# GpSimd's background instructions cut into pieces of at most 384 elements, in a fused H3 and squared-ReLU MLP kernel

## The chip, the cores and the metric

The kernel runs on one core of a Trainium2 chip. The metric is the device time of one execution in microseconds. Engines are named as in the profile: PE (TensorE, matrix products; PEld is its weight loads), DVE (VectorE), ACT (ScalarE), POOL (GpSimd) and SP (SyncE, which here issues every DMA from one queue, in order).

## The reference

Two layers, each of a block A (H3, a gated long convolution) and a block B (an MLP), in float32, with S = 2048 tokens, D = 1024 channels, F = 3584:

```
A(q):  k_shift = causal depthwise conv of k with shift_k (4 taps)
       kv = k_shift * v
       y  = causal conv of kv with ssm_k (2048 taps, per channel, by FFT) + kv * ssm_D
       return q * y
B(x):  h = x @ w1 + b1;  r = where(h > 0, h, 0);  h = r * r
       return h @ w2 + b2

x = q
for layer in 0, 1:
    x = x + A(layernorm(x))
    x = x + B(layernorm(x))
```

k, v and the filters do not depend on x, so the long convolution y is computed once and used in both layers.

## The kernel before, in words

Tokens come in four blocks b of 512. The work of the MLPs is a list of 8 units (layer, block) in the order (0,0), (1,0), (0,1), (0,2), (1,1), (0,3), (1,2), (1,3), called u0 to u7 here. A unit is a list of steps; one step uses one weight tile of 128x512 for 12 matmuls of 512 columns. Each float32 operand is split into a high and a low part, and a product is three matmuls (lines L336, L337, L338 of `mm3`).

Each step needs its weight tile `whl` split first: ACT copies the high part (`w_hi`, L1013), and the low part is a subtraction `wr - high` (`w_lo`, L1021) on DVE, or, where u0 passes into u1, three times in four on POOL. Split tiles of some weights are kept in DRAM (`wd_m...`) and come back by a DMA straight into `whl` (L1011). There are 6 `whl` buffers.

Beside the MLP steps runs the long convolution for blocks 1 to 3 (sb = 1, 2, 3), in the background. A transform (`fwd_x`, `fwd_g`, mostly ACT and DVE with some matmuls on PE; L366, L368, L484 and L485 are DVE's, L421 a transpose on PE) writes spectra to DRAM. `prod_stream` reads them into `cx` and `cg` and forms, for each of 16 channel groups, 3 kinds and 2 output positions per sb, the products of j+1 blocks of 128 elements: `mult` on POOL (L526) writes `cp` (3 buffers), and two products later in the program `red` on DVE (L530) sums it into `sm`. j is 2 and 3 for sb = 1, 4 and 5 for sb = 2, 6 and 7 for sb = 3. When a group's sums are there, POOL folds them (`fold`, L676) and makes a butterfly (L680, L681), and inverse matmuls on PE (L596, first stage) follow.

Near the start of each unit the bias b2 is loaded as a row over all partitions into a `px` buffer (2 buffers) and added by POOL to the accumulators that hold the residual: `add_b2` (L1744, four adds of 1024 elements) in u0 to u4, `add_b2w` (L1601, eight adds of 512) in u5 to u7. The `px` buffers also serve the loads of x for the next unit (`load_x`, L726).

The order of each engine's instructions is the order in which the program emits them: the step loop emits the MLP step and then, by a pace of products per step, background work. Only the first block (up to about 125 us) is ordered by a planner. So every engine works through a fixed queue, and an instruction that waits holds all behind it on the same engine; on SP that goes for DMA issues too.

Of the kernel before, what the change touches and what calls it, by code (L numbers as in the profile page):

```python
# [18 lines left out]
S, D, F = 2048, 1024, 3584  # L19
P = 128  # L20
# [7 lines left out]
BL = 256  # L28
# [15 lines left out]
NORM_0 = "VA"  # L44
AHEAD_0 = 4
BURST = 1.06
FIN = "GGG"
PACE_SLACK = {1: 74, 3: 10}
PACE_TO = {1: 2}
# [191 lines left out]
def tile_h3_mlp(ctx: ExitStack, tc: tile.TileContext, q, kT, vT, shk, ssmT, ssmD, w1, b1, w2, b2,  # L241
                fwd_t, pro_t, inv_t, sgn_t, out):
    nc = tc.nc
    V, A, G, PE, SY = nc.vector, nc.scalar, nc.gpsimd, nc.tensor, nc.sync
# [275 lines left out]
    def prod_stream():  # L520
# [2 lines left out]

        def mult(st, xt, gt, j):
            pr = cv.tile([P, CU, j + 1], F32, name="cp", bufs=3)
            G.tensor_mul(pr.rearrange("p c i -> p i c"), xt[:, 0:j + 1], gt[:, j::-1])  # L526
            st["pr"] = pr

        def red(st, sm, ty, jj):
# [2 lines left out]
        def fin(st, sm, sb, g, k):  # L532
            s = sm.rearrange("p k j c -> p k (j c)")
            E = ENG[FIN[sb - 1]]
            if k == 0:
                fold(E, s)
                lag.at(1, fin, st, sm, sb, g, 1)
            elif k == 1 and sb <= PLAIN:
# [100 lines left out]
        for n, (sb, g, ty) in enumerate(units):  # L639
            while n not in when:  # L640
                if (sb, g // 2) in fwd_done:
                    load(n)
                else:
                    lag.tick()
                    yield None
            while lag.n < when[n] + 2:
                lag.tick()
                yield None
            if ty == 0:
                while sums[0] - sums[1] >= 2:  # L650
                    lag.tick()
                    yield None
                sums[0] += 1
                sm = cv.tile([P, 3, BT, CU], F32, name="sm", bufs=2)
                if g % 2 == 0:
                    pair = {}
            for jj in range(BT):
                j = BT * sb + jj
                st = {"pair": pair}
                mult(st, *got[n], j)  # L660
                lag.at(2, red, st, sm, ty, jj)
                if jj == BT - 1:
                    if ty == 2:
                        lag.at(3, fin, st, sm, sb, g, 0)
                    fill(n)
                lag.tick()
                yield (j + 1) * CU * 1e-3
# [5 lines left out]
        return t[:, e].rearrange("p (n c) -> p n c", c=CG)  # L673

    def fold(E, s):
        E.tensor_add(s[:, 1:3], s[:, 1:3], s[:, 0:1].to_broadcast([P, 2, s.shape[2]]))  # L676

    def butterfly(E, s):
        y = s[:, 1:3].rearrange("p r (j u c) -> p u (r j) c", u=2, c=CG)
# [380 lines left out]
    def first_block():  # L1060
# [27 lines left out]
        with tc.tile_pool(name="pro", bufs=1) as pro:  # L1088
# [226 lines left out]
            def prods(c, jj):  # L1315
                sm = new(cv, "sm", 2, [P, 3, 2, CU])
                xs, gs = spec["x", c], spec["g", c]
                for ty in range(3):
                    rd = [(xs, ty), (gs, ty)]
                    if jj == 0:  # L1320
                        pl.add([("G", g_cost(BL), 1), ("V", v2_cost(BL), 1)], lambda e, ty=ty: ENG[e].tensor_mul(
                            sm.t[:, ty], xs.t[:, ty, :, 0], gs.t[:, ty, :, 0]), rd, [(sm, ty)])
                        continue
                    pr = new(cv, "fx", 4, [P, T])
                    pv = lambda t: t.rearrange("p (g b c) -> p g b c", g=2, b=BT)
                    pl.add([("G", g_cost(T), 1), ("V", v2_cost(T), 1)], lambda e, ty=ty, pr=pr: ENG[e].tensor_mul(
                        pv(pr.t), xs.t[:, ty], gs.t[:, ty, :, ::-1]), rd, [pr])
                    pl.add([("V", v2_cost(BL), 1), ("G", g_cost(BL), 1)], lambda e, ty=ty, pr=pr: ENG[e].tensor_add(
                        sm.t[:, ty], pv(pr.t)[:, :, 0], pv(pr.t)[:, :, 1]), [pr], [(sm, ty)])
                fl_ = lambda: sm.t.rearrange("p k g c -> p k (g c)")  # L1330
                pl.add([("G", g_cost(T), 1), ("V", v2_cost(T), 1)], lambda e: fold(ENG[e], fl_()),
                       [(sm, 0)], [(sm, 1), (sm, 2)])
                z = {}
                pl.add([("V", 2 * v2_cost(BL), 1), ("G", 2 * g_cost(BL), 1)], lambda e: z.update(
                    enumerate(butterfly(ENG[e], fl_()))), [], [(sm, 0), (sm, 1), (sm, 2)])
                behind(c, jj, sm, lambda: (z[0], z[1]), [(sm, 0), (sm, 1)])
# [261 lines left out]
    def add_b2w(st, wacc):  # L1598
        for j, h in ((1, 0), (2, 1), (3, 0), ("x", 1)):
            for a in wacc[j]:  # L1600
                G.tensor_add(a, a, st["t"][:, h * 512:(h + 1) * 512])  # L1601

    def evict_w(os, wacc, j, c):
        for n in range(2):
# [136 lines left out]

    def add_b2(st, accs):
        for a in accs:
            G.tensor_add(a, a, st["t"])  # L1744

    def store_out(accs, l, b):
        for tt in range(NT):
# [11 lines left out]
    for sb in range(1, NB):  # L1759
        if WIN[sb] > lo_u:  # L1760
# [3 lines left out]
            n = sum(last_step[u] + 1 - start_step[u] - 19 * (1 - PREP_PACE) for u in range(lo_u, hi_u))  # L1764
# [16 lines left out]
    for s, (k, u, c, a, i, tts, w) in enumerate(steps):  # L1781
# [3 lines left out]
        if u != cur_u:  # L1785
            cur_u = u
            if u:
                xT = nxt
            bst = {}
            if u in WINO:  # L1790
                wacc, rp = {}, {}
                lag.at(11, load_wacc, wacc, b)
                lag.at(34, load_b2, bst)
                lag.at(38, add_b2w, bst, wacc)
            else:
                if not (u and direct[u - 1]):
                    accs = []
                    lag.at(5, load_acc, accs, b)
                lag.at(12, load_b2, bst)
                lag.at(16, add_b2, bst, accs)  # L1800
# [10 lines left out]
        if k == "m1":  # L1811
# [9 lines left out]
            for kk in range(4):  # L1821
                t = slice(kk * P, (kk + 1) * P)
# [8 lines left out]
        elif k == "w2":  # L1831
# [7 lines left out]
            for n in range(2):  # L1839
                t = slice(n * P, (n + 1) * P)  # L1840
# [11 lines left out]
        else:  # L1852
# [5 lines left out]
            for tt in tts:  # L1858
                t = slice(tt * P, (tt + 1) * P)
# [33 lines left out]
        if u + 1 < NU and not direct[u]:  # L1893
            n = s - start_step[u]
# [23 lines left out]
        owed += rate  # L1918
        todo = min(owed, BURST * rate)
        while todo > 0:  # L1920
# [63 lines left out]
```

## Time and profile before

| | us |
|---|---|
| median of 3 runs | 2706.65 (2705.93 to 2711.74) |
| the profiled execution | 2710.68 |
| its span, first to last instruction | 2708.9 |
| PE busy | 2658.2 (98% of the span) |
| DVE busy | 1988.0 (73%) |
| ACT busy | 1124.1 (41%) |
| POOL busy | 845.8 (31%), 532 instructions |
| mean granted TensorE clock | 0.996 |

POOL's work lies almost wholly in the first 1700 us, where the convolution runs. PE is busy nearly all the time after the first 125 us, so the time is that of PE's work plus the places where PE stands still. Busy time of DVE and POOL includes time in which an instruction was started but held up.

### The profile page before, as it was taken

Reading aid. Unit: us, or ns where it says so; the run is one execution under the profiler, and the core shown is the slowest. Engines: PE = TensorE matmul, PEld = TensorE weight load, DVE = VectorE, ACT = ScalarE, POOL = GpSimd, SP = SyncE. Lnnn points to the kernel's source line nnn. Section 1 sums busy time; section 2 is a strip of 40 time slices with the busy share of each in tenths; the row PEclk is TensorE's granted clock in tenths of the full one; section 3 lists DMA queues with packets and bytes.
Section 4 is the critical chain, followed back from the end, with each engine's and each line's share of the span. In section 5 each row is a group of like instructions: output and inputs, shape, how many; then the busy total and the mean of one; then the engine's idle time right before and its main releaser. Section 6 shows DMA issues by size and latency. Waiting matters only on the chain.

```text
span 2708.9 us, 36533 instructions
## 1 busy us (share of the span) xinstructions
PE 2658.2 (98%) x12568; PEld 2227.5 (82%) x12568; DVE 1988.0 (73%) x3066; ACT 1124.1 (41%) x1936; POOL 845.8 (31%) x532
## 2 busy tenths in 40 slices
PE   7999999999999999999999999999999999999999
PEld 6888787888888888888888888888788788878887
DVE  7878888788987877779677765376787666664565
ACT  3454344433444233442234422244455444445443
POOL 2436565355632655236553454000000010001000
PEclk9999999999999999999999999999999999999999
DMA  8789898699999898788978887789888866676556
GB/s 250 262 305 314 290 311 279 234 308 372 333 305 321 300 342 285 266 334 289 354 263 276 298 304 248 237 295 310 294 286 300 278 231 212 231 270 210 179 167 206
DMA packets 377482, 755.05 MB, mean 279 GB/s; under 512 B 43840, under 2 KB 159184, under 8 KB 377296
## 3 DMA queue, kind: packets, MB, share of 16 engines
q1 hardware_dynamic: 377296, 752.72, 81.6%
q8 instruction: 99, 1.62, 0.2%
q14 instruction: 87, 0.71, 0.1%
HBM read 602.63 MB, written 149.95 MB: 278 GB/s over the span
## 4 chain that ended last, share of the span: by engine, by line
PE 82%; DMA 7%; DVE 6%; issue 2%; POOL 1%; ACT 1%; SPq 1%; DVEq 0%; ACTq 0%; POOLq 0%
PE p L336 25%; PE p L337 25%; PE p L338 25%; DMA wr<-w 2%; PE p L1097 2%; DVE whl L1021 1%; DMA whl<-wd_m 1%; PE pt L336 1%; PE pt L337 1%; PE pt L338 1%; DMA wd_m<-whl 1%; DMA whl<-wd_t 1%; DMA yt<-yd 0%; DMA wd_t<-whl 0%; DMA fx<-kT 0%
## 5 line engine op out<-in xcount | busy, mean ns | idle before, releaser
L526 POOL TENSOR_TENSOR cp<-cx,cg 128x384 f32<-128x384 f32 (+5 forms) x288 | 543.2, 1898 | 569.9 <-DVE sm L530 380.4
L336 PE MATMUL p<-xh,whl 128*128 128x512 f32 (+1 forms) x1840 | 707.6, 385 | 4.3 <-DMA whl<-wd_m 4.2
L338 PE MATMUL p<-xh,whl 128*128 128x512 f32 (+1 forms) x1840 | 703.8, 383 | 0.8 <-POOL whl L1021 0.8
L337 PE MATMUL p<-xl,whl 128*128 128x512 f32 (+1 forms) x1840 | 703.8, 383 | 0.1
L1013 ACT CAST whl<-wr 128x512 fp32r<-128x512 f32 x637 | 383.4, 619 | 437.0 <-PE p L338 308.5
L1021 DVE TENSOR_TENSOR whl<-wr,whl 128x512 fp32r<-128x512 f32 x622 | 500.9, 826 | 73.6 <-ACT whl L1013 69.2
L336 PE MATMUL p<-whl,rh 128*128 128x512 f32 x1372 | 541.2, 394 | 7.3 <-ACT whl L1013 3.7
L337 PE MATMUL p<-whl,rh 128*128 128x512 f32 x1372 | 536.6, 391 | 1.8 <-POOL whl L1021 0.8
L338 PE MATMUL p<-whl,rl 128*128 128x512 f32 x1372 | 536.0, 391 | 0.0
L336 PEld LDWEIGHTS p<-xh,whl 128*128 128x128 f32 x1840 | 347.0, 189 | 71.8 <-DMA whl<-wd_m 3.5
L338 PEld LDWEIGHTS p<-xh,whl 128*128 128x128 f32 x1840 | 346.6, 188 | 68.6 <-POOL whl L1021 1.0
L337 PEld LDWEIGHTS p<-xl,whl 128*128 128x128 f32 x1840 | 346.8, 188 | 65.6 <-DVE xl L1410 0.3
L336 PEld LDWEIGHTS p<-whl,rh 128*128 128x128 f32 x1372 | 258.7, 189 | 62.2 <-DMA whl<-wd_m 4.8
L337 PEld LDWEIGHTS p<-whl,rh 128*128 128x128 f32 x1372 | 258.7, 189 | 56.0 <-DVE whl L1021 3.4
L338 PEld LDWEIGHTS p<-whl,rl 128*128 128x128 f32 x1372 | 258.5, 188 | 54.3
L1504 DVE TENSOR_TENSOR rl<-wr,rh 128x512 fp32r<-128x512 f32 x140 | 145.8, 1042 | 178.3 <-ACT rh L1499 178.2
L1601 POOL TENSOR_TENSOR acc<-acc,px 128x512 f32<-128x512 f32 x18 | 23.2, 1325 | 766.6 <-DMA px<-b 766.6
L530 DVE TENSOR_REDUCE sm<-cp 128x128 f32<-128x384 f32 (+5 forms) x288 | 249.5, 874 | 10.9 <-POOL cp L526 10.9
L1496 ACT ACTIVATE wr<-p,b1t 128x512 f32<-128x512 f32 x138 | 95.2, 690 | 366.8 <-PE p L338 365.8
L1565 DVE TENSOR_TENSOR rl<-wr,rh 128x256 fp32r<-128x256 f32 x84 | 48.9, 582 | 211.2 <-ACT rh L1560 211.1
L1624 DVE TENSOR_TENSOR acc<-p,acc 128x512 f32<-128x512 f32 x152 | 99.8, 686 | 83.4 <-PE p L338 83.4
L1557 ACT ACTIVATE wr<-p,b1t 128x512 f32<-128x512 f32 x84 | 57.9, 689 | 191.0 <-PE p L338 190.9
(277 smaller groups left out, 3304.5 us busy)
## 6 DMA issues: line engine op xcount, KB each, us to landing
whl<-wd_m SPq DMA_DIRECT2D x379, 512.0 KB, 5.4
wr<-w SPq DMA_DIRECT2D x493, 256.0 KB, 5.4
wr<-td SPq DMA_DIRECT2D x152, 256.0 KB, 4.0
wd_m<-whl SPq DMA_DIRECT2D x70, 512.0 KB, 6.1
cx<-xd SPq DMA_DIRECT2D x48, 512.0 KB, 6.0
cg<-gd SPq DMA_DIRECT2D x48, 512.0 KB, 6.8
gd<-fg SPq DMA_DIRECT2D x72, 256.0 KB, 6.5
cx<-xd SPq DMA_DIRECT2D x48, 384.0 KB, 5.7
```

The costliest lines, as they stand in the source:

```text
L336: PE.matmul(o, lh, rh, start=start, stop=False)
L337: PE.matmul(o, lh, rl, start=False, stop=False)
L338: PE.matmul(o, ll, rh, start=False, stop=stop)
L526: G.tensor_mul(pr.rearrange("p c i -> p i c"), xt[:, 0:j + 1], gt[:, j::-1])
L530: V.tensor_reduce(sm[:, ty, jj], st["pr"], axis=AX.X, op=OP.add)
L1013: A.copy(t[:, 0], raws[n]["t"])
L1021: ENG[e[n % len(e)]].tensor_sub(t[:, 1], raws[n]["t"], t[:, 0].bitcast(F32))
L1097: PE.matmul(o, lh, r, start=start, stop=stop)
L1496: A.activation(r, st["o"], AF.Relu, bias=b1t[:, st["f"]:st["f"] + 1])
L1504: V.tensor_sub(st["lo"], st["r"]["t"], st["hi"].bitcast(F32))
L1557: A.activation(r, st["o"], AF.Relu, bias=b1t[:, st["f"]:st["f"] + 1])
L1624: V.tensor_add(accs[tt][:, d], o, accs[tt][:, d])
```

## The change

`mult` cuts a product of j+1 blocks into pieces of at most 3 blocks (384 elements): 3 blocks stay one instruction, 4, 5 and 6 blocks become two (2+2, 2+3, 3+3), 7 and 8 become three (2+2+3, 2+3+3). `fold` becomes two adds of 256 in place of one of 512. The adds of b2 are made in pieces of 256 (`BL`): four for each of 1024, two for each of 512. The arithmetic on each element is the same.

On POOL that is 336 more products, 48 more folds, and 60 and 24 more adds of b2: 468 instructions on top of 532. On every other engine and on SP the instructions and their order stay as they were, but for two folds of the first block that run on DVE and become four.

```diff
+G_BLOCKS = 3
...
         def mult(st, xt, gt, j):
             pr = cv.tile([P, CU, j + 1], F32, name="cp", bufs=3)
-            G.tensor_mul(pr.rearrange("p c i -> p i c"), xt[:, 0:j + 1], gt[:, j::-1])
+            n = -(-(j + 1) // G_BLOCKS)
+            cuts = [(j + 1) * k // n for k in range(n + 1)]
+            for a, e in zip(cuts, cuts[1:]):
+                G.tensor_mul(pr[:, :, a:e].rearrange("p c i -> p i c"), xt[:, a:e],
+                             gt[:, j - a:j - e if e <= j else None:-1])
             st["pr"] = pr
...
     def fold(E, s):
-        E.tensor_add(s[:, 1:3], s[:, 1:3], s[:, 0:1].to_broadcast([P, 2, s.shape[2]]))
+        for k in (1, 2):
+            E.tensor_add(s[:, k], s[:, k], s[:, 0])
...
     def add_b2w(st, wacc):
         for j, h in ((1, 0), (2, 1), (3, 0), ("x", 1)):
             for a in wacc[j]:
-                G.tensor_add(a, a, st["t"][:, h * 512:(h + 1) * 512])
+                for d in range(0, 512, BL):
+                    G.tensor_add(a[:, d:d + BL], a[:, d:d + BL], st["t"][:, h * 512 + d:h * 512 + d + BL])
...
     def add_b2(st, accs):
         for a in accs:
-            G.tensor_add(a, a, st["t"])
+            for d in range(0, D, BL):
+                G.tensor_add(a[:, d:d + BL], a[:, d:d + BL], st["t"][:, d:d + BL])
```

## The prediction

> **What bounds the kernel now.** I read the page first: it gives 2658.2 us of busy PE in a span of 2708.9, so the time is PE's work plus the places where PE stands still. Then the list of PE's waits, the granted clock in a few windows, and the timelines of PE, DVE, POOL and SP around the longest stalls. Rows of a list of waits read: who waited, for what, us in total, times, longest.
>
> ```profile
> PE 2658.2 (98%) x12568; PEld 2227.5 (82%) x12568; DVE 1988.0 (73%) x3066; ACT 1124.1 (41%) x1936; POOL 845.8 (31%) x532
> PE pt L421 <- DVE fx L368: 8.1, 3, 6.4
> PE p L336 <- DMA whl<-wd_m: 7.2, 6, 2.8
> PE pt L596 <- DVE fg L485: 2.7, 1, 2.7
> PE p L338 <- POOL whl L1021: 0.8, 1, 0.8
> DVE sm L530 <- POOL cp L526: 10.9, 15, 1.6
> ```
>
> After the first block PE waits little, and for DVE and DMA rather than for POOL. A change on POOL therefore acts through three doors: how long POOL holds up DVE, how late DVE gets what POOL makes, and how late SP gets a buffer that POOL frees. The last row is the second door: small, but there.
>
> A stall costs more than its length, because the clock falls behind it. Windows (length, busy time of PE, PEld, DVE, ACT and POOL, granted clock, DMA):
>
> ```profile
> 300.05 1.10 PE L421 MATMUL pt<-ident,fx 128*128 128x128 f32 x4 [6.36 <-DVE fx L368]
> 295.87:306.10 10.23, 6.05 (x17) 4.92 (x18) 9.74 (x14) 1.49 (x3) 6.73 (x6) 0.50 0.88 281
> 446.05:449.46 3.41, 3.41 (x13) 2.83 (x12) 3.38 (x7) 0.39 (x1) 2.60 (x2) 0.50 0.00 0
> 1910.36:1913.78 3.42, 3.42 (x10) 2.65 (x9) 0.00 (x0) 0.00 (x0) 0.00 (x0) 0.50 0.94 347
> ```
>
> Behind the 6.36 us stall PE runs at half speed until 306.10, 6.05 us of running, so 3.0 us are lost on top. The second window follows the 2.67 us stall of L596 (2.7 in the list), the third the 2.81 us one: 3.4 us at 0.50, 1.7 us lost each. I call the first two A (9.4 us in all) and B (4.4 us).
>
> **What a cut costs on POOL.** The same add in three lengths (duration min/median/max in ns), and two starts in a row:
>
> ```profile
> L681 POOL TENSOR_TENSOR sm<-sm x49: 725/742/1255, 109.2 to 1692.0; 128x256 f32<-128x256 f32 x49
> L1601 POOL TENSOR_TENSOR acc<-acc,px x18: 1277/1292/1540, 1891.7 to 2486.4; 128x512 f32<-128x512 f32 x18
> L1744 POOL TENSOR_TENSOR acc<-acc,px x20: 2383/2842/2877, 164.5 to 1553.4; 128x1024 f32<-128x1024 f32 x20
> 432.62 0.74 POOL L681 TENSOR_TENSOR sm<-sm 128x256 f32<-128x256 f32 x1
> 433.31 1.31 POOL L526 TENSOR_TENSOR cp<-cx,cg 128x512 f32<-128x512 f32 x1
> ```
>
> Two of 256 take 1450 ns where one of 512 takes 1277: 0.17 us more by duration. But the 0.74 us instruction is followed after 0.69, so starts overlap ends by 0.05: a cut costs 0.12 us where POOL runs on without a break. The 468 cuts add 56 us to 846 of POOL. The larger cost stands beside it: at each boundary a waiting DVE instruction may go in between. L1744's median lies 0.46 us above its minimum, which I read as that.
>
> **What a cut gives to DVE.** The low-part subtraction, all of DVE's 622:
>
> ```profile
> L1021 DVE TENSOR_TENSOR whl<-wr,whl x622: 673/685/2909, 145.3 to 2697.4; 128x512 fp32r<-128x512 f32 x156
> ```
>
> The longest exceeds the shortest by 2.24 us, about one POOL instruction of 1024. So a DVE instruction with two SBUF inputs waits for the POOL instruction that is under way, and goes next. In pieces of 256 and 384 that wait falls to 0.7 or 1.0 us at most. The Trainium skill's page "SBUF — State Buffer", section "Who interferes with whom", says that the pair of ports shared by the two engines is taken for a whole instruction by whichever issues first while the other blocks fully, also for a DVE instruction with two SBUF inputs against a POOL one that reads SBUF. The trace agrees, with those 2.24 us; the rule speaks for the change, and what it would make of the time is the second rival.
>
> **The long products (sb = 2 and 3, 550 to 1700 us): nothing.** They hold most of the cuts (288), but:
>
> ```profile
> L526 POOL TENSOR_TENSOR cp<-cx,cg 128x768 f32<-128x768 f32 (+2 forms) x193 | 415.5, 2159 | 479.0 <-DVE sm L530 357.0 <-DMA cg<-gd 110.9 <-DMA kd<-fk 6.4
> ```
>
> In that window POOL idles 479 us before products, 357 of them until DVE has emptied a buffer. POOL runs ahead, so 288 x 0.12 = 35 us plus handovers of up to 0.46 us each (132 us) fit in, and PE's longest waits lie elsewhere, so DVE's gain buys nothing. If the cover were gone, DVE's sums would come late and hold the split weights behind them.
>
> **Place 1: b2 adds at the head of u1.** POOL, DVE, then PE (start, length, engine and line, idle before):
>
> ```profile
> 531.84 10.86 POOL L1744 TENSOR_TENSOR acc<-acc,px 128x1024 f32<-128x1024 f32 x4
> 542.65 1.73 POOL L1021 TENSOR_TENSOR whl<-wr,whl 128x512 fp32r<-128x512 f32 x1
> 532.45 2.36 DVE L1504 TENSOR_TENSOR rl<-wr,rh 128x512 fp32r<-128x512 f32 x1 [5.30 <-ACT rh L1499]
> 534.73 2.90 DVE L1021 TENSOR_TENSOR whl<-wr,whl 128x512 fp32r<-128x512 f32 x1
> 537.55 5.69 DVE L1504 TENSOR_TENSOR rl<-wr,rh 128x512 fp32r<-128x512 f32 x2
> 543.17 1.76 DVE L1021 TENSOR_TENSOR whl<-wr,whl 128x512 fp32r<-128x512 f32 x1
> 544.43 0.38 PE L338 MATMUL p<-xh,whl 128*128 128x256 f32 x1 [0.83 <-POOL whl L1021]
> ```
>
> Here POOL also makes a weight's low part, queued behind the adds, and PE is already waiting 0.83 us for it. Four adds alone are 4 x 2.38 - 3 x 0.05 = 9.4 us; the row has 10.86, so three handovers at 0.49. Sixteen pieces alone are 16 x 0.725 - 15 x 0.05 = 10.85. DVE no longer loses about 2 us per instruction, so the five DVE instructions shown can all go in where three did: 5 x 0.46 = 2.3. Together 13.2 against 10.9: L1021 comes 2.3 to 2.4 us later, and PE stands 3.2 us instead of 0.83. That is longer than the 2.67 us that brought half clock, so 1.7 more: **+4.1 us**. With no more handovers than now it is +1.5 without clock loss, with seven +5.
>
> The Trainium skill's page "TensorE: Matmul & The Clock Gate", section "HAM oscillation — how this bites in real kernels", states as its rule that there be no idle gap of PE above about 3.4 us. By it, 3.2 us would pass without a slower clock, and the sum below would be 1.7 us lower. The trace differs, with half clock behind 2.67 us, and I go by the trace.
>
> **Place 2: b2 adds in u5; place 3: in u6.** SP's queue (SPq) issues a load of x into the `px` buffer that holds b2, so it stands until the last add, and the weight loads stand behind it (the first row is of SP's waits):
>
> ```profile
> SPq L726 <- POOL fk L1601: 18.1, 2, 10.0
> 1891.71 7.72 POOL L1601 TENSOR_TENSOR acc<-acc,px 128x512 f32<-128x512 f32 x6 [199.01 <-DMA px<-b]
> 1899.38 2.99 POOL L1601 TENSOR_TENSOR fk<-fk,px 128x512 f32<-128x512 f32 x2
> 1902.40 0.32 SPq L726 DMA_DIRECT2D px<-x  x1
> 1902.82 1.36 SPq L1011 DMA_DIRECT2D whl<-wd_m  x1
> 1909.27 0.50 PE L336 MATMUL p<-xh,whl 128*128 128x512 f32 x1 [2.81 <-DMA whl<-wd_m]
> 2199.76 0.32 SPq L726 DMA_DIRECT2D px<-x  x1
> 2204.76 0.19 PEld L336 LDWEIGHTS p<-xh,whl 128*128 128x128 f32 x1 [0.29 <-DMA whl<-wd_m]
> ```
>
> The adds end at 1902.37, SP goes on at 1902.40, and the load lands as PE starts at 1909.27 after 2.81 us. Eight more cuts are 8 x 0.12 = 1.0 us, and one more handover makes 1.3. That reaches PE whole: a stall of 4.1 us. Its half clock lies between the 1.7 us of the 2.8 us stall (no more than now) and the 3.0 of A; I take 0.8 more. **+2.1 us**, from +1.0 to +3. In u6 PEld waits 0.29 us for the load behind the same step, so there is no slack left: **+1.2 us**, from +0.8 to +1.6, below the stalls that move the clock. u7 loads no further unit.
>
> **The first convolution stage (sb = 1, 190 to 490 us): about even.** Stalls A and B lie here. Before A:
>
> ```profile
> 291.66 3.69 DVE L366 SCALAR_TENSOR_TENSOR fx<-fx,shkt 128x512 f32<-128x512 f32 x3
> 295.27 1.21 DVE L484 TENSOR_TENSOR fg<-fk 128x256 f32<-128x256 f32 x1
> 296.41 1.49 DVE L485 TENSOR_TENSOR fg<-fk 128x256 f32<-128x256 f32 x1
> 297.82 1.48 DVE L1021 TENSOR_TENSOR whl<-wr,whl 128x512 fp32r<-128x512 f32 x1
> 291.23 1.30 POOL L676 TENSOR_TENSOR sm<-sm 128x512 f32<-128x512 f32 x1 [3.71 <-DVE sm L530]
> 294.77 3.98 POOL L526 TENSOR_TENSOR cp<-cx,cg 128x384 f32<-128x384 f32 x3
> ```
>
> The fold holds L366 from 291.66 to 292.53; cut, to 291.96, so 0.6 us come free. But the second half is one more turn for POOL, and the three products that hold L484, L485 and L1021 (0.8 us for the last: 1.48 against 0.67) have 384 elements and stay whole. So A keeps nearly all of its 6.36 us. In this stage only the products of 512 and the folds are cut, half the instructions; what DVE saves there it partly gives back in waiting for `cp` (10.9 us in 15 waits, above). I take **-1 us**, from -14 (A and B gone) to +6. The cut adds in u0 (about 165 us) lie where PE has no stall: nothing. Two DVE folds in the first block: under 0.2 us.
>
> **Sum.** +4.1 + 2.1 + 1.2 - 1.0 = +6.4 us, set against the profiled execution's 2710.68 (span 2708.9 and 1.8 around it): 2717.1. That execution lies 4.0 above the median of the runs; the differences should hold for the median as well: 2706.65 + 6.4 = **2713.0**.
>
> **The rivals.** *POOL too slow in the first stage* (slower still): cut products of 512 cost 0.12 + 0.46 us each; where DVE already waits for `cp`, that goes to DVE. Five of the waits in the approach to A and B would be 5 x 0.58 = 2.9 us more stall, and about 3 us of clock: 2713.0 + 6 = 2719. For it, the 15 waits; against it, POOL idles there too. Chance 0.18.
>
> *The locks decide* (faster): by the whole-instruction hold, DVE loses half as much at each meeting. If that carries back through the 100 us ahead of A, DVE meets its dates: A (9.4) and B (4.4) go, 13.8 us, less half of the three places' cost (3.7): 2696.6; with A gone alone and the three places in full, 2704.7. It decides from 3.7 us of DVE time saved ahead of A, since stalls below 2.67 us are the only ones seen without a clock loss. Against it, the uncut 384s. Chance 0.24.
>
> *All hidden* (no change): DVE's earlier instructions make up for POOL's later ones at place 1, DMA timing swallows places 2 and 3: 2706 to 2709. Chance 0.16. That the change does not do what it says has no place here: POOL's queue holds the pieces, and other queues are in their old order.
>
> **Chances.** The forecast has 0.42. About 0.2% (5.4 us) is what a measurement can tell from no change. The forecast's bounds reach from +2 to +10, 0.30 above the line and 0.12 within; the first rival is slower; the locks faster by more than 0.2% in 0.22 and within it in 0.02; the last within. Slower 0.48, same 0.30, faster 0.22. Range: from 2698, leaving out the lower part of the locks' case, to 2722, the first rival with its clock loss in full.
>
> **What would show it.** Right: L1021 on POOL after the adds at the head of u1 starts 2 to 3 us later against them, with PE waiting about 3 us for POOL; the waits of SP's L726 for POOL's L1601 rise from about 18 to 21 us, and stalls before `whl<-wd_m` grow; L1021's longest on DVE falls to about 1.7 us; A still there. Wrong: A or B gone, place 1's stall unchanged, or new stalls of PE between 550 and 1700 us.

## The result and the profile after

The changed kernel takes 2715.94 us (median of 8 runs, 2712.03 to 2718.89) against 2707.78 us (8 runs, 2705.93 to 2711.74) for the kernel before on the same chip: ratio 1.0029, 95% interval 1.0018 to 1.004, that is 8.2 us slower, from 4.9 to 10.8. The forecast was 2713.0 us, slower by 6.4. In the changed kernel lines of the second half are numbered some more: L421 is L422, L526 is L530, L530 is L535, L596 is L601, L626 is L631, L726 is L732, L1011 is L1017, L1021 is L1027, L1504 is L1510, L1601 is L1608, L1744 is L1752, and L336 to L338 are L337 to L339.

The profiled execution took 2713.12 us (span 2711.3), near the lowest of this kernel's runs, while that of before (2710.68) was near the highest of its own. So the two traces differ by only 2.4 us where the medians differ by 8.2. A trace can show here where PE stands; sums are taken from the timed runs. First the page: engines, then groups (busy us, mean ns | idle us before them).

```profile
PE 2659.8 (98%) x12568; PEld 2229.0 (82%) x12568; DVE 1891.6 (70%) x3068; ACT 1126.2 (42%) x1936; POOL 950.7 (35%) x1000
L530 POOL TENSOR_TENSOR cp<-cx,cg 128x384 f32<-128x384 f32 (+1 forms) x624 | 622.0, 1029 | 503.7 <-DVE sm L535 288.8
L1027 DVE TENSOR_TENSOR whl<-wr,whl 128x512 fp32r<-128x512 f32 x622 | 470.9, 778 | 78.0 <-ACT whl L1019 75.6
L535 DVE TENSOR_REDUCE sm<-cp 128x128 f32<-128x384 f32 (+5 forms) x288 | 250.1, 875 | 40.2 <-POOL cp L530 40.2
```

DVE is busy 96.4 us less than before (1988.0), because its subtractions are held up for a shorter time (the low part takes 778 ns on the mean, 826 before; the sums, with 875 and 874 ns, gain nothing); POOL is busy 104.9 us more (845.8). DVE's wait for products rose from 10.9 to 40.2 us (most of it behind the adds of b2, see e7 and e8). None of the three shows in PE's busy time, 2659.8 against 2658.2. The list of PE's waits (total, times, longest) and the spread of DVE's low-part subtraction (ns, least/median/longest):

```profile
PE p L337 <- DMA whl<-wd_m: 9.6, 10, 2.2
PE pt L422 <- DVE fx L369: 7.2, 1, 7.2
PE p L339 <- POOL whl L1027: 3.5, 1, 3.5
PE pt L601 <- DVE fg L486: 2.3, 1, 2.3
```

```profile
L1027 DVE TENSOR_TENSOR whl<-wr,whl x622: 673/686/1548, 144.8 to 2699.5; 128x512 fp32r<-128x512 f32 x156
```

So DVE's longest hold fell from 2909 to 1548 ns, as the cut into shorter POOL instructions should make it; but the two stalls that DVE is to blame for, A (7.2 against 6.4) and B (2.3 against 2.7), are still there, and the wait for POOL's L1027 grew from 0.8 to 3.5 us. Place 1 in the timelines of POOL, DVE and PE (start, length, instruction, idle before):

```profile
528.68 14.32 POOL L1752 TENSOR_TENSOR acc<-acc,px 128x256 f32<-128x256 f32 x16
542.96 1.26 POOL L1027 TENSOR_TENSOR whl<-wr,whl 128x512 fp32r<-128x512 f32 x1
```

```profile
529.29 0.69 DVE L1510 TENSOR_TENSOR rl<-wr,rh 128x512 fp32r<-128x512 f32 x1 [5.02 <-ACT rh L1505]
530.26 0.87 DVE L1027 TENSOR_TENSOR whl<-wr,whl 128x512 fp32r<-128x512 f32 x1 [0.28 <-ACT whl L1019]
532.17 0.80 DVE L1510 TENSOR_TENSOR rl<-wr,rh 128x512 fp32r<-128x512 f32 x1 [1.04 <-ACT rh L1505]
535.00 1.23 DVE L1510 TENSOR_TENSOR rl<-wr,rh 128x512 fp32r<-128x512 f32 x1 [2.03 <-ACT rh L1505]
536.15 1.23 DVE L1027 TENSOR_TENSOR whl<-wr,whl 128x512 fp32r<-128x512 f32 x1
537.93 1.28 DVE L1510 TENSOR_TENSOR rl<-wr,rh 128x512 fp32r<-128x512 f32 x1 [0.55 <-ACT rh L1505]
539.14 0.54 DVE L535 TENSOR_REDUCE sm<-cp 128x128 f32<-128x384 f32 x1
540.77 0.97 DVE L1510 TENSOR_TENSOR rl<-wr,rh 128x512 fp32r<-128x512 f32 x1 [1.09 <-ACT rh L1505]
```

```profile
544.27 0.58 PE L339 MATMUL p<-xh,whl 128*128 128x256 f32 x1 [3.54 <-POOL whl L1027]
```

The adds take 14.32 us where they took 10.86. DVE no longer suffers: it is often idle, waiting for ACT. Its eight instructions all go in between the sixteen pieces, and POOL pays for it. What PE waits for is POOL's own subtraction, behind the last piece. Windows of after (length; busy PE, PEld, DVE, ACT, POOL; granted clock; DMA), the first behind this stall, the others behind stalls of 2.31 us (B) and 2.16 us (before `whl<-wd_m`, PE resumes at 629.27):

```profile
542.80:549.70 6.90, 5.43 (x18) 4.75 (x19) 1.47 (x3) 2.22 (x4) 6.90 (x9) 0.51 0.08 30
443.80:447.30 3.50, 3.50 (x11) 2.77 (x10) 3.47 (x6) 0.50 (x2) 2.42 (x3) 0.51 0.01 2
626.00:633.00 7.00, 4.84 (x22) 3.70 (x22) 4.17 (x6) 3.68 (x8) 5.96 (x7) 1.00 1.05 381
```

At place 1 PE runs 5.43 us at half clock, 2.7 us lost; with 3.54 - 0.83 = 2.7 us more standing, 5.4 in all. Both traces hold the same matmuls in the same order, so the starts of each can be compared, and they say nearly the same: after is 2.9 us ahead of before when the stall begins and comes out 2.3 behind, 5.2 in all.

Places 2 and 3, from the waits and timelines of after:

```profile
SPq L732 <- POOL fk L1608: 21.0, 2, 11.4
1896.31 8.56 POOL L1608 TENSOR_TENSOR acc<-acc,px 128x256 f32<-128x256 f32 x12 [200.17 <-DMA px<-b]
1904.84 2.81 POOL L1608 TENSOR_TENSOR fk<-fk,px 128x256 f32<-128x256 f32 x4
1907.67 0.32 SPq L732 DMA_DIRECT2D px<-x  x1
1908.10 0.37 SPq L1017 DMA_DIRECT2D whl<-wd_m  x1
1912.68 0.50 PE L337 MATMUL p<-xh,whl 128*128 128x512 f32 x1 [2.16 <-DMA whl<-wd_m]
2208.10 0.19 PEld L337 LDWEIGHTS p<-xh,whl 128*128 128x128 f32 x1 [1.90 <-DMA whl<-wd_m]
```

SP's wait did rise from 18.1 to 21.0 us. In u6 (last row) PEld's wait for the load rose from 0.29 to 1.90 us. But in u5 the stall became shorter, 2.16 us against 2.81: the load was issued 1908.10 - 1896.31 = 11.8 us after the start of the adds, not 11.1, yet PE went on 4.58 us after the issue, not 6.45.

### The profile page after: what moved, and what is told of

The parts are those of the page before. It is cut to its first block, busy times and chain, and to the rows that moved or that the text cites. A ratio compares the mean times of both kernels' runs of the same rounds, so it can differ in the third digit from the quotient of the medians.

```text
span 2711.3 us, 36967 instructions
## 1 busy us (share of the span) xinstructions
PE 2659.8 (98%) x12568; PEld 2229.0 (82%) x12568; DVE 1891.6 (70%) x3068; ACT 1126.2 (42%) x1936; POOL 950.7 (35%) x1000
## 4 chain that ended last, share of the span: by engine, by line
PE 76%; DMA 10%; DVE 6%; POOL 4%; issue 2%; SPq 1%; ACT 1%; DVEq 0%; POOLq 0%; ACTq 0%
PE p L338 23%; PE p L337 23%; PE p L339 23%; PE p L1103 2%; DMA whl<-wd_m 2%; DMA cg<-gd 2%; POOL cp L530 2%; DVE whl L1027 1%; DMA gd<-fg 1%; DMA wr<-w 1%; POOL acc L1752 1%; PE pt L339 1%; PE pt L337 1%; PE pt L338 1%; DMA wd_m<-whl 1%
## 5 line engine op out<-in xcount | busy, mean ns | idle before, releaser
L530 POOL TENSOR_TENSOR cp<-cx,cg 128x384 f32<-128x384 f32 (+1 forms) x624 | 622.0, 1029 | 503.7 <-DVE sm L535 288.8
L337 PE MATMUL p<-xh,whl 128*128 128x512 f32 (+1 forms) x1840 | 708.6, 385 | 7.4 <-DMA whl<-wd_m 7.3
L339 PE MATMUL p<-xh,whl 128*128 128x512 f32 (+1 forms) x1840 | 704.2, 383 | 3.5 <-POOL whl L1027 3.5
L338 PE MATMUL p<-xl,whl 128*128 128x512 f32 (+1 forms) x1840 | 704.2, 383 | 0.1
L337 PE MATMUL p<-whl,rh 128*128 128x512 f32 x1372 | 541.2, 394 | 5.9 <-ACT whl L1019 3.4
L338 PE MATMUL p<-whl,rh 128*128 128x512 f32 x1372 | 536.2, 391 | 1.6 <-POOL whl L1027 0.8
L339 PE MATMUL p<-whl,rl 128*128 128x512 f32 x1372 | 535.8, 391 | 0.0
L1027 DVE TENSOR_TENSOR whl<-wr,whl 128x512 fp32r<-128x512 f32 x622 | 470.9, 778 | 78.0 <-ACT whl L1019 75.6
L337 PEld LDWEIGHTS p<-xh,whl 128*128 128x128 f32 x1840 | 347.3, 189 | 76.3 <-DMA whl<-wd_m 4.9
L339 PEld LDWEIGHTS p<-xh,whl 128*128 128x128 f32 x1840 | 347.1, 189 | 71.2 <-POOL whl L1027 3.7
L338 PEld LDWEIGHTS p<-xl,whl 128*128 128x128 f32 x1840 | 347.3, 189 | 65.6 <-DVE xl L1416 0.3
L337 PEld LDWEIGHTS p<-whl,rh 128*128 128x128 f32 x1372 | 258.7, 189 | 60.7 <-ACT whl L1019 4.2
L338 PEld LDWEIGHTS p<-whl,rh 128*128 128x128 f32 x1372 | 258.6, 188 | 56.1 <-DVE whl L1027 3.2
L339 PEld LDWEIGHTS p<-whl,rl 128*128 128x128 f32 x1372 | 258.3, 188 | 54.3
L1608 POOL TENSOR_TENSOR acc<-acc,px 128x256 f32<-128x256 f32 x36 | 25.7, 750 | 763.8 <-DMA px<-b 763.8
L535 DVE TENSOR_REDUCE sm<-cp 128x128 f32<-128x384 f32 (+5 forms) x288 | 250.1, 875 | 40.2 <-POOL cp L530 40.2
L1510 DVE TENSOR_TENSOR rl<-wr,rh 128x512 fp32r<-128x512 f32 x140 | 118.3, 845 | 214.1 <-ACT rh L1505 213.8
```

What stands on the lines that cost most here:

```text
L337: PE.matmul(o, lh, rh, start=start, stop=False)
L338: PE.matmul(o, lh, rl, start=False, stop=False)
L339: PE.matmul(o, ll, rh, start=False, stop=stop)
L530: G.tensor_mul(pr[:, :, a:e].rearrange("p c i -> p i c"), xt[:, a:e], gt[:, j - a:j - e if e <= j else None:-1])
L535: V.tensor_reduce(sm[:, ty, jj], st["pr"], axis=AX.X, op=OP.add)
L1027: ENG[e[n % len(e)]].tensor_sub(t[:, 1], raws[n]["t"], t[:, 0].bitcast(F32))
```

## The experiments

Ratios are to the kernel before, timed on the same chip in the same rounds (medians 2707.95, 2709.77 and 2709.40 us in the three sets: e1 to e4, e5 to e8, e9 to e12), with 95% intervals.

### Which part costs: e1, e2, e3, e4

**e1**, the changed kernel with `add_b2` whole again:

```diff
-            for d in range(0, D, BL):
-                G.tensor_add(a[:, d:d + BL], a[:, d:d + BL], st["t"][:, d:d + BL])
+            G.tensor_add(a, a, st["t"])
```

> The changed kernel with the adds of 1024 left whole again (products, folds and the adds of u5 to u7 still cut). Theory, that the cut adds at the head of u1 delay a weight's low part that POOL makes behind them: the stall of PE there falls from 3.54 us to about 0.8, its half clock goes, and with them about 5.4 us: 2710.5, from 2709 to 2712. Rival, that the shorter products and folds cost the time through a POOL that is late in the convolution: 2715 to 2717, as the changed kernel.

**e2**, the kernel before with only this cut made (the same lines the other way round).

> The kernel before with the adds of 1024 alone cut into four. Theory (adds at the head of u1): that stall of PE grows from 0.83 us to 3 us or more with half clock behind it, 4 to 5.5 us: 2712 to 2713.5 against 2707.8. Rival (products): within 1 us of the kernel before.

**e3**, the kernel before with only the products cut (`mult` as in the change; folds and adds whole).

> The kernel before with the products alone cut. Theory: DVE is held less in the first convolution stage, PE gains 1 to 3 us up to 490 us, as the changed kernel's trace shows (3.4 us ahead there, part of it from the folds), and may lose 2 or 3 us to a late DMA near 620 us: 2705 to 2709. Rival (POOL late in the convolution): slower by 5 us or more, 2713 and up, with DVE waiting longer for the products.

**e4**, the kernel before with only `add_b2w` cut, in pieces of 256.

> The kernel before with the eight adds of 512 in u5 to u7 alone cut into two. Theory (they hold SP's queue, and the weight loads behind it): the adds end 1 us later, PE's stall at 1906 us grows by 1.0 to 1.3 us and one of 1.0 to 1.5 us appears at 2204: 2709 to 2711. Rival, that the load's landing is set by DMA traffic and not by its issue: within 0.7 us of the kernel before.

| | us | ratio |
|---|---|---|
| changed kernel | 2715.94 | 1.0029 (1.0018 to 1.0040) |
| e1, all but the cut of `add_b2` | 2710.59 | 1.0007 (0.9998 to 1.0016) |
| e2, the cut of `add_b2` alone | 2712.03 | 1.0015 (1.0006 to 1.0024) |
| e3, the products alone | 2707.78 | 0.9998 (0.9989 to 1.0006) |
| e4, the cut of `add_b2w` alone | 2710.22 | 1.0007 (0.9998 to 1.0016) |

Place 1 in the timelines of e1 and of e2, POOL then PE:

```profile
526.51 10.86 POOL L1751 TENSOR_TENSOR acc<-acc,px 128x1024 f32<-128x1024 f32 x4
539.10 0.39 PE L339 MATMUL p<-xh,whl 128*128 128x256 f32 x1 [0.83 <-POOL whl L1027]
```

```profile
528.63 14.43 POOL L1745 TENSOR_TENSOR acc<-acc,px 128x256 f32<-128x256 f32 x16
544.33 0.39 PE L338 MATMUL p<-xh,whl 128*128 128x256 f32 x1 [3.65 <-POOL whl L1021]
```

With the adds whole the stall is back at 0.83 us though everything else is cut; with them cut it is 3.65 us though everything else is whole. The cut of `add_b2` by itself makes the kernel 0.15% slower, 4.1 us (1.6 to 6.5), and without it the changed kernel can't be told from before. This is the largest part, and it lies at place 1. e3 shows that the products, 336 of the 468 added instructions, cost nothing that can be measured. e4's interval reaches no change, so its 1.9 us (0.0007 of 2707.95) rest on its trace, where place 3 is seen again:

```profile
2204.70 0.19 PEld L336 LDWEIGHTS p<-xh,whl 128*128 128x128 f32 x1 [1.55 <-DMA whl<-wd_m]
```

The parts together make 0.15 + 0.07 - 0.02 = 0.20%, the whole 0.29% (0.18 to 0.40). The difference lies within the intervals; the folds weren't run alone. Taken out of the changed kernel (e1) the cut of `add_b2` is worth 0.29 - 0.07 = 0.22%, put into the kernel before (e2) 0.15%.

### Who must not stand behind the adds: e5, e6

All low parts between u0 and u1 are made on DVE, so that POOL makes none behind its adds; e5 does this to the changed kernel, e6 to the one before.

```diff
-WLO = {"b": "GGGV", "x": "GGGV"}
+WLO = {"b": "GGGV", "x": "V"}
```

> The changed kernel, with the weights' low parts at the passage from u0 to u1 all made by DVE (three in four were POOL's). All pieces stay cut. Theory (a weight queued behind the cut adds on POOL): PE no longer waits for POOL there, the 3.5 us stall and its half clock go, 4 to 6 us: 2710 to 2712. Rival (the cut adds cost through DVE, which their many small pieces hold up): PE waits for DVE's L1021 there instead, 2714 to 2717.

> The same move of the low parts in the kernel before, whose adds of 1024 are whole. Theory: there is only a stall of 0.83 us to take away at that place, and DVE is held up to 2.4 us by each add: 2706 to 2710, no gain that can be measured. Rival (the move itself is a gain anywhere): 2703 to 2705.

e5: 2713.49 us, 1.0016 (1.0006 to 1.0025). e6: 2709.14 us, 0.9998 (0.9989 to 1.0007). All of e5's waits of PE between 500 and 700 us that the list has:

```profile
PE p L337 <- DMA whl<-wd_m: 2.8, 1, 2.8
PE pt L339 <- DVE whl L1027: 1.4, 1, 1.4
```

The wait for POOL is gone, as the theory of place 1 says, and a shorter one for DVE (1.4 us) takes its place; e6 has the same 1.4 us. The ratio of the cut kernel fell from 1.0029 to 1.0016, so about half of the loss went with POOL's place in that queue. By the starts of the same matmuls from 500 to 560 us, the changed kernel loses 5.2 us on the kernel before, e2 4.5, and e5, e6 and e1 nothing: in these traces the loss at place 1 went whole. What remains of e5's 0.16% lies elsewhere in its trace, where PE stands 2.8 us near 625 us and PEld 2.6 us at place 3. It is more than e1 leaves, but the two intervals overlap.

### The products apart: e7, e8

**e7** cuts only the products of sb = 1 (`n = ... if j < 4 else 1` in `mult`), **e8** only those of sb = 2 and 3 (`if j >= 4 else 1`); all else is as before.

> The kernel before with only the products of 512 (sb = 1, 190 to 560 us) cut. If cutting helps DVE in the first convolution stage: 2704 to 2707. If it makes POOL late there (as one rival of the prediction had it): 2710 to 2714. If both are small: 2707 to 2709, and no stall before a weight load near 620 us above the 0 to 1.6 us of kernels with whole products.

> The kernel before with only the products of 640 to 1024 (sb = 2 and 3, from 560 us on) cut. The prediction held these for nothing: 2707 to 2709. The traces with all products cut show a stall of PE of 2.2 to 2.4 us near 620 us before a weight load that stands behind a load for the products in SP's queue: if it comes from these cuts it is here too, and the time is 2709 to 2712.

e7: 2708.46 us, 0.9999 (0.9990 to 1.0008). e8: 2710.58 us, 1.0003 (0.9994 to 1.0012). Neither moves the time, so the nothing of e3 isn't a gain in one stage against a loss in the other. (e8's 2710.58 us lies in the range expected with a stall near 620 us, but the kernel before took 2709.77 in this set, and the stall in e8 is 0.72 us.) A is 6.6 us in e7, 6.0 in e8, 5.0 in e3; over all fourteen traces it goes from 5.0 to 7.3, in no order with what is cut. DVE's waits for products rise to 15.1 us in e7, 12.9 in e8 and 20.4 in e3. The first row is e3's, the second e2's, where every product is whole:

```profile
DVE sm L535 <- POOL cp L530: 20.4, 29, 2.5
DVE sm L530 <- POOL cp L526: 30.0, 20, 6.9
```

The cut of products makes twice the 10.9 us of before, at no cost to PE that can be measured; I take it that the waits end before a weight is late, since the program takes up a product two products after it is made. The larger part of the changed kernel's 40.2 us is not theirs: e1, with the products cut and the adds of b2 whole, has 16.7 us, and the longest waits (6.9 in e2, 7.2 in after) are for products that stand behind the cut adds near 1230 us. They cost PE nothing either: from 1000 to 1250 us it waits 0.2 us in after and 0.5 in before.

### How much per piece: e9

**e9** is the kernel before with `add_b2` in pieces of 512 (eight instead of four or sixteen).

```diff
-            G.tensor_add(a, a, st["t"])
+            for d in range(0, D, 512):
+                G.tensor_add(a[:, d:d + 512], a[:, d:d + 512], st["t"][:, d:d + 512])
```

> The kernel before with the adds of 1024 alone cut into two of 512 (not four of 256). A dose of the first theory: eight adds take 8 x 1.28 - 7 x 0.05 = 9.9 us alone, and four to six handovers of 0.46 us make 11.7 to 12.6 us where four whole adds take 10.86 and sixteen pieces 14.3 to 14.4. PE's stall for the weight behind them is 1.7 to 2.6 us (0.83 whole, 3.5 in quarters); with half clock behind it if it passes about 2.3 us: 2708.5 to 2711.5 against about 2708.5 for the kernel before. Rival (any cut there costs the full amount, by what it does to DVE): 2712 and more.

2712.02 us, 1.0006 (0.9996 to 1.0016): just above the range expected in us, and as a ratio between before and e2, with an interval that reaches both. So the time alone doesn't decide between the theory and its rival. The timeline of e9 is clearer:

```profile
529.44 12.80 POOL L1745 TENSOR_TENSOR acc<-acc,px 128x512 f32<-128x512 f32 x8
543.97 0.39 PE L338 MATMUL p<-xh,whl 128*128 128x256 f32 x1 [2.47 <-POOL whl L1021]
```

Four, eight and sixteen pieces take 10.86, 12.80 and 14.43 us, and PE stands 0.83, 2.47 and 3.65 us: the stall follows the adds, less a part (3.57 us of adds, 2.82 of stall), which I put down to DVE's earlier instructions; no run shows that apart. From 500 to 560 us e9 loses 3.2 us by the starts of the same matmuls, where e2 loses 4.5: a dose, and not the full amount.

### SP's queue behind b2w: e11, e10, e12

**e11** is the kernel before with `add_b2w` in pieces of 128, to see whether SP's wait reaches PE when it is long enough.

```diff
-                G.tensor_add(a, a, st["t"][:, h * 512:(h + 1) * 512])
+                for d in range(0, 512, 128):
+                    G.tensor_add(a[:, d:d + 128], a[:, d:d + 128], st["t"][:, h * 512 + d:h * 512 + d + 128])
```

> The kernel before with the adds of 512 in u5 to u7 cut into four of 128 (the change cuts them into two): a larger dose at the same place. 32 pieces of about 0.41 us from start to start are 13.1 us against 10.0 for eight whole ones. Theory (SP's queue): the stalls before weight loads in u5 and u6 grow by about 3 us each less what the load gains by landing sooner, and a stall above 2.3 us in u6 brings half clock: 2712 to 2717. Rival (DMA traffic): 2708 to 2711, as with halves.

2720.85 us, 1.0040 (1.0027 to 1.0053), above the range expected. From the waits and the timeline of e11:

```profile
SPq L726 <- POOL fk L1602: 29.1, 2, 15.6
1892.64 11.28 POOL L1602 TENSOR_TENSOR acc<-acc,px 128x128 f32<-128x128 f32 x24 [199.50 <-DMA px<-b]
1903.88 5.09 POOL L1602 TENSOR_TENSOR fk<-fk,px 128x128 f32<-128x128 f32 x8
1913.98 0.80 PE L336 MATMUL p<-xh,whl 128*128 128x512 f32 x1 [7.08 <-DMA whl<-wd_m]
2214.83 0.79 PE L336 MATMUL p<-xh,whl 128*128 128x512 f32 x1 [5.19 <-DMA whl<-wd_m]
```

The adds end 16.3 us after their start (before: 10.7), and PE stands 7.08 us in u5 and 5.19 in u6. So the path from POOL's adds through the `px` buffer and SP's queue to the weights is real, and both places are on it.

**e10** takes the wait away by loading and adding b2 sooner in u5 to u7, when neither the next x nor its loads are due (the kernel before, adds whole):

```diff
-                lag.at(34, load_b2, bst)
-                lag.at(38, add_b2w, bst, wacc)
+                lag.at(18, load_b2, bst)
+                lag.at(22, add_b2w, bst, wacc)
```

> The kernel before with the load and the adds of b2 in u5 to u7 made 16 steps earlier, before the loads of x for the next unit; lengths as before. Theory (the adds hold a buffer, a load of x waits for it in SP's queue, and weight loads wait behind that): SP no longer waits for POOL there, the stall of 2.8 us in u5 and its half clock go (up to 4.5 us): 2703.5 to 2706 against about 2708.5. Rival (the weight load is late by DMA traffic): within 1.5 us of the kernel before.

2724.33 us, 1.0054 (1.0041 to 1.0067): the expected gain became a loss. Its waits of PE from 1850 us to the end:

```profile
PE p L337 <- DVE whl L1021: 9.3, 6, 2.8
PE p L336 <- DVE acc L1608: 4.2, 2, 2.2
PE p L336 <- DMA whl<-wd_m: 2.9, 5, 1.0
```

The same window in the list of DVE's waits:

```profile
DVE acc L1608 <- POOL acc L1601: 9.6, 4, 4.9
```

PE's waits for the load did shrink: 2.9 us here, 7.2 in the kernel before, and SP no longer waits for POOL's adds. But in these units DVE adds results (L1608) into the same accumulators; it now finds POOL still at them and waits, and the split weights (L1021) wait behind it on DVE. The kernel before has no wait of DVE for POOL in this window. What I had taken for slack in the accumulators was not there: one queue's wait was exchanged for another's.

**e12** is the changed kernel with both remedies, `add_b2` whole as in e1 and the early adds of e10.

> The changed kernel with products, folds and the adds of u5 to u7 still cut, the adds of 1024 whole, and the load and adds of b2 in u5 to u7 made 16 steps earlier. If the change costs its time at those adds alone, this stands with the kernel before or ahead of it by the stalls that go in u5 and u6: 2703.5 to 2708.5. If the cuts of products and folds cost time of their own: 2710 and more.

2727.42 us, 1.0072 (1.0057 to 1.0087), for the same reason, and worse, since the cut adds that DVE waits for take longer. Its waits of PE and of DVE from 1850 us on:

```profile
PE p L338 <- DVE whl L1027: 9.5, 4, 3.4
PE p L337 <- DVE acc L1615: 7.8, 3, 2.9
```

```profile
DVE acc L1615 <- POOL acc L1608: 17.0, 6, 6.2
```

No version beat the kernel before. e1, e3, e4, e6, e7, e8 and e9 can't be told from it.

## Why the prediction was right, and where its terms were off

**Place 1 (+4.1): the right mechanism, its terms somewhat small, the size right by the timed runs.** L1027 on POOL starts 14.28 us after the first add, against 10.81 before: 3.5 us later, where 2.3 to 2.4 was forecast. The step at fault is the count of handovers: not five but the eight DVE instructions shown above went in, since DVE, freed of its long holds, got through three more while the adds ran. With the sum of the prediction that is (14.32 - 10.85) / 8 = 0.43 us each, close to its 0.46 (0.50 if the one sum among the eight, L535, is left out). The stall was 3.54 us (forecast 3.2) and the clock loss 2.7 in this trace (forecast 1.7), so 5.4 us, just over the bound of +5. The timed value is e2's 4.1 us (1.6 to 6.5), or about 6 by way of e1.

**Place 2 (+2.1, from +1 to +3): wrong.** Here the prediction said that 1.3 us more of adds "reaches PE whole". Twelve traces show otherwise. The stall in u5 before `whl<-wd_m`, and the time from the issue of that load to PE's start:

| `add_b2w` | stall in u5, us | issue to PE's start, us |
|---|---|---|
| whole: before, e2, e3, e6, e7, e8, e9 | 2.81, 1.45, 2.46, 2.18, 2.43, 3.09, 1.95 | 6.45, 5.52, 5.83, 5.83, 5.79, 6.63, 5.80 |
| in 256: after, e1, e4, e5 | 2.16, 2.52, 2.00, 1.98 | 4.58, 4.58, 4.62, 4.57 |
| in 128: e11 | 7.08 | 4.57 |

The stall's mean is 2.34 us with whole adds and 2.17 with adds in 256: no growth. Counted from the start of the adds, the load is issued after 11.1 us in all seven kernels with whole adds, after 11.8 in after and e4 and 12.6 in e1 and e5. So the adds' delay is 0.7 or 1.5 us, about the 1.3 forecast, and none of it reaches PE: the time from issue to PE's start is shorter instead, 4.6 us against 5.5 to 6.6. Of e11's delay of 5.7 us, 4.7 come through. The prediction had treated 6.45 us, the one row it had, as the length of the load; with 4.6 us in five other traces, the row seems to hold a wait for something else as well. What that is, the runs don't show (the DMA engines' share between issue and PE's start doesn't tell them apart: 0.84 in before and 0.78 in e8, 0.76 in after and 0.79 in e11).

**Place 3 (+1.2, from +0.8 to +1.6): right.** PEld's wait for the same load in u6 is 0.29 us in before, 1.10 in e6, 0.64 in e7, 0.46 in e9 and not there in e2, e3 and e8; with the adds in 256 it is 1.90 (after), 1.95 (e1), 1.55 (e4) and 2.63 (e5). The means are 0.36 and 2.01: 1.6 us, the upper end of the forecast. The load has no slack to give here. In e5 half clock came on top (0.52 behind a stall of PE of 2.20 us), which the forecast didn't reckon with.

**The first convolution stage (-1) and the long products (nothing): right within what can be measured**, by e7 (0.9999) and e8 (1.0003). A and B stayed, as forecast, in every kernel. One thing was missed: with all products cut a stall before `whl<-wd_m` near 625 us appears, 2.16 us in after, 2.21 in e1, 2.42 in e3, 2.82 in e5 and 1.90 in e12. SP's queue, which issues that load, waits there for POOL to empty a buffer that the products read; the list of its waits in after, 610 to 630 us:

```profile
SPq L631 <- POOL cp L530: 5.7, 1, 5.7
```

That wait is not the whole cause: e8 has one of 6.0 us there and e2 one of 5.5, without such a stall. In the other kernels the stall is 0.1 to 1.35, but for e11, which has no cut product and still shows 2.16. With half the products cut it is 0.41 (e7) and 0.72 (e8). The prediction called new stalls there a sign of being wrong. By the starts of the same matmuls from 605 to 645 us this one costs 2.1 us in after, and up to 4.2 (e5) in the others of the five. Whether that is part of the changed kernel's time is open: e3 as timed lost nothing, but its trace, with the stall, is of the slowest of its 11 runs (2711.81 us; the next is 2708.36), and the other ten may not have it. Why it appears in e11 is open too.

**The rival that the locks decide** fell: DVE lost 96 us of held-up time, its longest subtraction went from 2909 to 1548 ns, and A and B stayed. The section "Who interferes with whom" of the Trainium skill's page "SBUF — State Buffer", by which DVE and POOL shut each other out for a whole instruction, agrees with those 2909 and 1548 ns; the other half of such an exchange, what it costs POOL, decided here. **POOL too slow in the first stage**: up to 500 us, DVE's waits for products rose only from 10.9 to 14.7 us (14.2 in e7), and the price didn't come (e7).

**The clock.** The prediction had half clock behind a stall from 2.67 us up. The runs show no such limit: see the last section.

The sum: 4.1 forecast and 4.1 measured at place 1, 3.3 forecast and 1.9 (-0.5 to 4.3) measured for places 2 and 3 together, and for the products -0.5 (-3.0 to +1.6) where -1 was forecast. By parts 5.5 us, forecast 6.4, measured on the whole 8.2 (4.9 to 10.8). The prediction's total owes something to errors that offset each other: place 2 was too large, place 1's clock loss too small in the trace. The 2.7 us between the parts and the whole can't be placed: they lie within the intervals, and most of them is the difference between the two ways of pricing the cut of `add_b2`, by e2 or by e1.

## What to carry to other kernels

To cut an instruction of one engine so that another gets in sooner is paid for on the first engine, at each boundary, and by whatever stands behind it in that queue; before cutting, look at what that is. Cut background work that has slack (here the products: no cost, no gain), not a run of adds with a weight or a buffer release behind it. And the time saved on an engine that is not late anywhere, 96 us of DVE's here, buys nothing until a stall is found that it ends.

## What the runs showed of the hardware

**Landing time.** The load of `whl` in u5 took 4.57 to 4.62 us from issue to use in the five kernels that issued it late (11.8 us or more after the start of the adds), and 5.5 to 6.6 in the seven that issued it early (11.1 us). Why is not shown.

**Clock.** Half clock follows stalls of about 2 us in some cases and not in others. In the changed kernel alone, the windows quoted above have 0.51 behind 2.31 us and 1.00 behind 2.16 us. In e1 1.91 us was followed by 0.57 over the next 4.0 us, while in e3 2.05 us was followed by 1.00 over 3.6 us. So no single length separates the two here, and the windows don't show what else does. The Trainium skill's page "TensorE: Matmul & The Clock Gate", section "HAM oscillation — how this bites in real kernels", asks for no idle gap above about 3.4 us; the rows here put the risk lower.
